# Copying the second half of w_in on VectorE instead of by DMA, each piece placed behind the work that it follows in time

## The chip, the cores and the metric

The kernel runs on one core of one Trainium2 chip. The metric is the device time of one execution in microseconds (us). A profile gives the span from the first to the last instruction, which is about 1.7 us shorter than the time of the same execution. Engines: PE is TensorE (matmuls), PEld its weight loads, DVE is VectorE, ACT is ScalarE, POOL is GpSimd, SP is SyncE, which here only issues DMAs. The kernel's matmuls write their results into tiles in PSUM; copying them from there into tiles in SBUF is called eviction below.

In the views below, rows left out are marked by "...".

## The reference, cut to what matters

A causal convolution of 7 taps over the sequence (weights by softmax, one set for each of 8 groups of 24 channels), then an MLP with the activation h * sigmoid(beta * h):

```python
# x: 8 x 4096 x 192, weight: 8 x 7
out = np.einsum('hk,bskhg->bshg', softmax(weight), windows_of_7(x))
x = out.reshape(32768, 192)
h = x @ w_in                                  # 192 x 2048
g = h * (1.0 / (1.0 + np.exp(-beta * h)))
return g @ w_out                              # 2048 x 192
```

## The kernel before: the parts that the change touches

The 192 channels are cut into NG = 3 chunks of 64. Two halves of the batch are worked on together: partitions 0 to 63 hold a chunk of the first half, partitions 64 to 127 the same chunk of the second. The kernel keeps w_in in SBUF twice, once for each set of partitions, and its matmuls read w_in from the same partitions as x. It is loaded in four pieces of 512 columns from HBM into partitions 0 to 63 (GpSimd issues these DMAs and they cast to bf16), and then copied inside SBUF to partitions 64 to 127. Piece 0 is copied by VectorE; pieces 1 to 3 by DMAs that SyncE issues.

```python
NW = 4
FW = F // NW                                   # 512 columns a piece
w_in_s = consts.tile([128, NG, F], BF16)

def load_w_in(i):
    cols = slice(i * FW, (i + 1) * FW)
    nc.gpsimd.dma_start(out=w_in_s[0:DG, :, cols], in_=moe_w_in[:, cols]...)

def second_w_in(i):
    cols = slice(i * FW, (i + 1) * FW)
    return dict(out=w_in_s[DG : 2 * DG, :, cols], in_=w_in_s[0:DG, :, cols])

load_w_in(0)
# ... cut ...
load_x(nc.gpsimd, x1b, TOK, 0, NB)
for i in range(1, NW):
    load_w_in(i)
    nc.sync.dma_start(**second_w_in(i))        # waits for load_w_in(i)
# ... w_out loads, cut; later, in VectorE's order:
nc.vector.tensor_copy(**second_w_in(0))
```

The main loop works in steps. Step s computes the hidden block `hidden(s, u)` for u = 0 to 15 (128 columns of w_in each, so blocks 4, 8 and 12 are the first to need pieces 1, 2 and 3) and, between them, the output of step s - 1. VectorE computes the convolution of a later step as 21 "taps" (`tensor_scalar` for the first of each chunk, `scalar_tensor_tensor` for the others). In step 0 there is no output yet; some start-up work is put between its hidden blocks:

```python
def hidden(s, fc):
    ph = psum_h.tile([128, 2, TOK], FP32, name="ph")       # 2 buffers
    for j in range(NG):
        for h in range(2):                                 # h = 1 reads the copied half
            rows = slice(h * DG, (h + 1) * DG)
            nc.tensor.matmul(ph[:, h, 0:n], w_in_s[rows, j, cols], cts[s][rows, j, 0:n], ...)
    nc.scalar.activation(gs[s][:, fc, :, 0:n], ph[:, :, 0:n], AF.Silu, scale=beta[:, fc : fc + 1])

first_work = {
    1: more(xt1_work),      # transposes of the next chunk of x, on TensorE
    3: more(xt1_work),      # the rest of them, and VectorE takes them out of PSUM
    5: more(conv1_work),    # convolution of step 1, one chunk of channels, on TensorE
    8: more(conv1_work),
    11: more(conv1_work),   # the last chunk, and VectorE takes it out of PSUM
}
```

GpSimd scales w_out by 1/beta (`prep_w_out`, four operations of 128x768) during step 0. The kernel gives each engine its instructions as one stream, in the order in which they were written.

## Time and profile before

| | before |
|---|---|
| time, median of 3 runs | 706.83 us (706.76 to 709.17) |
| span of the profiled run | 705.6 us |
| TensorE busy | 688.8 us, 98% |
| VectorE, ScalarE busy | 547.4 us, 577.8 us |
| longest wait of TensorE | 7.68 us, at 15.35 us |

From the page of the kernel before, the busy times of the engines and the group of the hidden matmuls (columns: line, engine, operation, output<-inputs, shapes, count; then busy us and mean ns; then idle time before them and what ended most of it):

```profile
PE 688.8 (98%) x11465; PEld 529.3 (75%) x11465; DVE 547.4 (78%) x932; ACT 577.8 (82%) x543; POOL 70.5 (10%) x83
L364 PE MATMUL ph<-ct,w_in_s 64*128 64x512 bf16 (+1 forms) x3168 | 427.0, 370 | 9.8 <-DMA w_in_s<-w_in_s 7.7
```

TensorE is the limit, and it idles 705.6 - 688.8 = 16.8 us in all. The second line says where nearly half of that is: 7.7 us in front of hidden matmuls, ended by the DMA that copies w_in from w_in.

The timeline of TensorE of the kernel before, start-up and the beginning of step 1 (start us, duration us, engine, line, what, count, and idle time before it):

```profile
14.61 0.53 PE L237 MATMUL po<-ident_b,x1b 128*64 128x128 bf16 x12
15.07 0.28 PE L364 MATMUL ph<-ct,w_in_s 64*128 64x256 bf16 x1
23.04 1.46 PE L364 MATMUL ph<-ct,w_in_s 64*128 64x256 bf16 x11 [7.68 <-DMA w_in_s<-w_in_s]
24.43 1.86 PE L250 MATMUL po<-xt_148,diag 128*128 128x256 f32 x7
...
28.25 1.10 PE L250 MATMUL po<-xt_148,diag 128*128 128x256 f32 x7
...
34.60 0.50 PE L364 MATMUL ph<-ct,w_in_s 64*128 64x256 bf16 x6 [0.20 <-ACT g L371]
34.92 0.51 PE L395 MATMUL po<-w_out_s,g 64*128 64x192 bf16 x8
```

At 15.07 the fifth hidden block (u = 4) issues one matmul, which needs only the first half of piece 1, and then stands for 7.68 us. Note the two convolution chunks: 1.86 us after the hole, 1.10 us later for the same seven matmuls. Step 1 begins at 34.60.

The table by stretches of the kernel before explains the 1.86 us (stretch; length, then busy us and instruction count of PE, PEld, DVE, ACT, POOL; then the granted TensorE clock, the DMA share and GB/s):

```profile
15.00:17.00 2.00, 0.35 (x7) 0.09 (x1) 1.78 (x5) 0.41 (x1) 0.00 (x0) 0.92 1.02 309
17.00:19.00 2.00, 0.00 (x0) 0.00 (x0) 2.00 (x3) 0.00 (x0) 1.82 (x1) 0.50 1.10 317
23.00:25.00 2.00, 1.97 (x13) 1.30 (x14) 0.00 (x0) 1.11 (x2) 2.00 (x2) 0.50 1.02 69
25.00:27.00 2.00, 2.00 (x17) 1.58 (x16) 0.00 (x0) 0.22 (x1) 2.00 (x3) 0.52 1.03 66
27.00:29.00 2.00, 1.56 (x20) 1.16 (x15) 0.00 (x0) 1.91 (x3) 2.00 (x4) 1.00 2.14 144
```

The granted clock falls to 0.50 in the hole and stays there until about 27, so the first 4 us of work after the hole run at a granted clock of 0.50. This is counted as busy time, not as waiting.

The timeline of VectorE of the kernel before:

```profile
9.97 0.76 DVE L286 COPY w_in_s<-w_in_s 64x1536 bf16<-64x1536 bf16 x1
...
15.18 0.96 DVE L315 COPY xt<-po 128x1536 bf16<-128x1536 bf16 x1 [2.92 <-PE po L237]
16.18 0.88 DVE L345 TENSOR_SCALAR ct<-xt,cw 128x512 bf16<-128x512 bf16 x3
16.97 2.62 DVE L347 SCALAR_TENSOR_TENSOR ct<-xt,cw,ct 128x512 bf16<-128x512 bf16 x2
32.14 0.96 DVE L301 CAST ct<-po 128x768 bf16<-128x768 f32 x1 [12.56 <-PE po L250]
```

A copy of one piece by VectorE takes 0.76 us; the same copy by DMA took 8.8 us to landing (median of three, table of DMA issues). VectorE idles from 19.6 to 32.1.

The chain of work that ended last, before, in order of time, passes the same stretch by another way:

```profile
10.23 12.57 DMA w_out_raw<-in_moe_w_out_dram
22.88 1.41 POOL w_out_s L321
24.28 3.54 DMA xd<-in_x_dram
27.82 0.49 PE ph L364 x6
```

It names the loads of w_out and of x and not the copy of w_in. Its link at 27.82 is a TensorE wait of 0.44 us that was put down to a DMA of x, which a hidden matmul does not read. The chain is inferred from semaphore events, and one wrong link sends everything before it astray. So "the DMA engines are too busy for w_out and x" is a rival reading of this profile.

### The profile page before, as it was taken

How to read it: one execution, taken by the hardware profiler on the slowest of the kernel's cores; microseconds unless marked ns; L12 is line 12 of the kernel's file. 1: busy time of each engine (PE TensorE's matmuls, PEld its weight loads, DVE VectorE, ACT ScalarE, POOL GpSimd, SP SyncE). 2: the span in 40 equal slices, each digit the busy share in tenths (PEclk: the TensorE clock that was granted, in tenths of full speed). 3: DMA queues.
4: the chain of work that ended last, by engine and by line, in shares of the span. 5: the costliest groups of instructions: out<-in, count | busy, mean ns of one | idle time of the engine just before them, and what ended most of it. 6: DMA issues, size and time to landing. Idle time of an engine off the chain costs nothing.

```text
span 705.6 us, 24846 instructions
## 1 busy us (share of the span) xinstructions
PE 688.8 (98%) x11465; PEld 529.3 (75%) x11465; DVE 547.4 (78%) x932; ACT 577.8 (82%) x543; POOL 70.5 (10%) x83
## 2 busy tenths in 40 slices
PE   7699999999999999999999999999999999999996
PEld 5487777777777777777777777777777777777776
DVE  5299999999798877788877779877778887777213
ACT  4499888888888888888888888888888888888881
POOL 6954544000000000000000000000000000000000
PEclk9799999999999999999999999999999999999999
DMA  9999999922212221421223220232221322111011
GB/s 178 155 161 161 159 168 177 139 57 60 69 44 51 69 71 47 69 59 35 69 70 49 69 69 32 63 69 65 52 70 48 47 69 70 47 47 47 24 47 69
DMA packets 182073, 55.16 MB, mean 78 GB/s; under 512 B 146432, under 2 KB 181648, under 8 KB 181968
## 3 DMA queue, kind: packets, MB, share of 16 engines
q0 software_dynamic: 98048, 14.89, 29.9%
q1 hardware_dynamic: 83872, 38.68, 24.3%
q8 instruction: 89, 1.46, 0.8%
q14 instruction: 16, 0.13, 0.1%
q10 hardware_dynamic: 48, 0.01, 0.0%
HBM read 28.98 MB, written 37.29 MB: 94 GB/s over the span
## 4 chain that ended last, share of the span: by engine, by line
PE 95%; DMA 2%; POOL 1%; ACT 0%; issue 0%; DVE 0%; POOLq 0%
PE po L395 48%; PE ph L364 47%; DMA w_out_raw<-in_moe_w_out_dram 2%; DMA xd<-in_x_dram 1%; ACT g L371 0%; POOL w_in_s L142 0%; POOL w_out_raw L185 0%; PE po L250 0%; POOL x1b L117 0%; POOL w_out_s L321 0%; DVE osb L404 0%; DVE osb L405 0%; POOL sel L158 0%; POOL sel L167 0%; POOL sel L156 0%
## 5 line engine op out<-in xcount | busy, mean ns | idle before, releaser
L371 ACT ACTIVATE g<-ph,beta 128x1024 bf16<-128x1024 f32 (+1 forms) x528 | 571.5, 1088 | 106.2 <-PE ph L364 102.3
L395 PEld LDWEIGHTS <-g 64*128 64x128 bf16 x8192 | 370.2, 94 | 101.3 <-issue 0.4
L364 PE MATMUL ph<-ct,w_in_s 64*128 64x512 bf16 (+1 forms) x3168 | 427.0, 370 | 9.8 <-DMA w_in_s<-w_in_s 7.7
L395 PE MATMUL po<-w_out_s,g 64*128 64x192 bf16 x8192 | 430.3, 243 | 0.2 <-issue 0.2
L347 DVE SCALAR_TENSOR_TENSOR ct<-xt,cw,ct 128x512 bf16<-128x512 bf16 x558 | 380.6, 747 | 0.0
L364 PEld LDWEIGHTS <-w_in_s 64*128 64x128 bf16 x3168 | 164.1, 94 | 63.5 <-DMA w_in_s<-w_in_s 7.9
L404 DVE COPY osb<-po 128x384 f32<-128x384 f32 x128 | 71.4, 558 | 129.3 <-PE po L395 123.3
L405 DVE TENSOR_TENSOR osb<-po,osb 128x384 f32<-128x384 f32 x128 | 71.4, 558 | 4.4
L95 POOL DMA_DIRECT2D xd<-in_x_dram x60 | 54.3, 906 | 49.6 <-DMA xd<-in_x_dram 46.5
L345 DVE TENSOR_SCALAR ct<-xt,cw 128x512 bf16<-128x512 bf16 x93 | 27.5, 349 | 0.0
L301 DVE CAST ct<-po 128x768 bf16<-128x768 f32 x1 | 1.0, 958 | 12.6 <-PE po L250 12.6
L321 POOL TENSOR_TENSOR w_out_s<-w_out_raw,beta_r 128x768 bf16<-128x768 f32 x4 | 6.6, 1674 | 3.1 <-DVE ct L345 2.6
L250 PE MATMUL po<-xt_148,diag 128*128 128x256 f32 x28 | 5.2, 332 | 0.0
L205 PE MATMUL ph<-zeros 128*128 128x512 bf16 x8 | 3.8, 625 | 1.3 <-DVE warm L132 1.3
L250 PEld LDWEIGHTS po<-xt_148,diag 128*128 128x128 f32 x28 | 4.3, 223 | 0.9 <-issue 0.8
L250 PEld LDWEIGHTS ph<-xt_148,diag 128*128 128x128 f32 x14 | 2.9, 303 | 0.7 <-ACT xt_148 L271 0.6
L250 PE MATMUL ph<-xt_148,diag 128*128 128x256 f32 x14 | 3.4, 406 | 0.0
L315 DVE COPY xt<-po 128x1536 bf16<-128x1536 bf16 x1 | 1.0, 958 | 2.9 <-PE po L237 2.9
L185 POOL DMA_DIRECT2D w_out_raw<-in_moe_w_out_dram x4 | 3.1, 789 | 0.0
L262 ACT CAST ct<-po 128x256 bf16<-128x256 f32 x1 | 0.4, 372 | 3.1 <-PE po L250 3.1
L205 PEld LDWEIGHTS <-zeros 128*128 128x128 bf16 x8 | 0.9, 129 | 2.5 <-issue 1.3
L142 POOL DMA_DIRECT2D w_in_s<-in_moe_w_in_dram x4 | 2.6, 676 | 0.8 <-POOLq L464 0.8
(45 smaller groups left out, 26.3 us busy)
## 6 DMA issues: line engine op xcount, KB each, us to landing
out_dram<-osb SPq DMA_DIRECT2D x62, 384.0 KB, 3.0
xd<-in_x_dram POOLq DMA_DIRECT2D x54, 198.0 KB, 14.7
w_out_raw<-in_moe_w_out_dram POOLq DMA_DIRECT2D x4, 384.0 KB, 9.9
xd<-in_x_dram POOLq DMA_DIRECT2D x6, 192.0 KB, 14.6
x_83<-in_x_dram SPq DMA_DIRECT2D x4, 192.0 KB, 4.0
w_in_s<-in_moe_w_in_dram POOLq DMA_DIRECT2D x4, 192.0 KB, 7.9
out_dram<-osb SPq DMA_DIRECT2D x4, 192.0 KB, 5.8
w_in_s<-w_in_s SPq DMA_DIRECT2D x3, 192.0 KB, 8.8
```

The costliest lines, as they stand in the source:

```text
L95: nc.gpsimd.dma_start(out=xd[r0:, :, h, :], in_=x_v[p, t0:t1, h, :].rearrange("t (c d) -> t c d", c=NG),)
L185: nc.gpsimd.dma_start(out=w_out_raw[:, c : c + 4, :], in_=w_out_v[:, c : c + 4, :])
L205: nc.tensor.matmul(pf[:, 0, :], zeros[:, 0:128], zeros, start=True, stop=True)
L250: nc.tensor.matmul(pv, diag[:, c, k, :], xt0[:, c, o : o + n], start=(k == 0), stop=(k == K - 1),)
L321: nc.gpsimd.tensor_tensor(w_out_s[:, c0 : c0 + n, :], w_out_raw[:, c0 : c0 + n, :], beta_r[:, c0 : c0 + n].unsqueeze(2).to_broadcast((128, ...
L345: nc.vector.tensor_scalar_mul(dst, src, scalar)
L347: nc.vector.scalar_tensor_tensor(out=dst, in0=src, scalar=scalar, in1=dst, op0=ALU.mult, op1=ALU.add)
L364: nc.tensor.matmul(ph[:, h, 0:n], w_in_s[rows, j, cols], cts[s][rows, j, 0:n], start=(j == 0), stop=(j == NG - 1),)
L371: nc.scalar.activation(gs[s][:, fc, :, 0:n], ph[:, :, 0:n], AF.Silu, scale=beta[:, fc : fc + 1])
L395: nc.tensor.matmul(po[:, r, b * D : (b + 1) * D], g[rows, fc, h, q * BLK : (q + 1) * BLK], w_out_s[rows, fc, :], start=(fc == 0), stop=(fc ...
L404: nc.vector.tensor_copy(dst, po[:, 0, 0 : 2 * D])
L405: nc.vector.tensor_tensor(dst, po[:, 1, 0 : 2 * D], dst, ALU.add)
```

## The change

Intent: take the second DMA out of the path. VectorE copies a piece in under 1 us. As VectorE works in order, each copy is placed where its piece should have landed: copy 1 behind the first transposes (u = 1), copy 2 behind the eviction of the transposes (u = 3), copy 3 at u = 5.

```diff
-    def second_w_in(i):
+    def copy_w_in(i):
         cols = slice(i * FW, (i + 1) * FW)
-        return dict(out=w_in_s[DG : 2 * DG, :, cols], in_=w_in_s[0:DG, :, cols])
+        nc.vector.tensor_copy(w_in_s[DG : 2 * DG, :, cols], w_in_s[0:DG, :, cols])
@@
     for i in range(1, NW):
         load_w_in(i)
-        nc.sync.dma_start(**second_w_in(i))
@@
-    nc.vector.tensor_copy(**second_w_in(0))
+    copy_w_in(0)
@@
-        1: more(xt1_work),
-        3: more(xt1_work),
-        5: more(conv1_work),
+        1: lambda: (more(xt1_work)(), copy_w_in(1)),
+        3: lambda: (more(xt1_work)(), copy_w_in(2)),
+        5: lambda: (more(conv1_work)(), copy_w_in(3)),
```

## The prediction

> **What bounds the kernel.** TensorE: the page gives it 688.8 us busy of 705.6 (98%), and the table by stretches shows no idle time from 50 to 700 us, at a granted clock of 1.00. So only the first 45 us can be won. The one large hole is at 15.35 us: the timeline shows the fifth hidden block's first matmul at 15.07 and the next at 23.04, after 7.68 us of waiting (list of waits) for the DMA that copies the second half of w_in, piece 1. SyncE issued it at 13.40, when piece 1 itself had landed; it took about 9.6 us. The hole costs more than itself: the granted clock is 0.50 from 17 to about 27 us. [...]
>
> **Removed, added, moved.** Three DMA copies of 192 KB go (median 8.8 us to landing). Three VectorE copies like the one already there come: 0.76 us each (timeline), 2.3 us together. VectorE works in order:
> - copy 1 waits for piece 1 (13.4) and ends near 14.2, before the work it feeds (15.1); it holds up only a halo cast and the transposes' eviction, which can't start before 15.18.
> - copies 2 and 3 follow that eviction (ends 16.14): to about 16.9 and 17.7, or 1 to 2 us later. Their pieces have landed by 16; their readers come near 18 and 22.
> - then five convolution taps (16.2 to 19.6 before). VectorE had idled from 19.6 to 32.1, so there is room.
>
> **On the critical path.** TensorE goes on at 15.07 at full clock. From pieces of the trace at full clock: two hidden blocks to 16.1; one convolution chunk to the next 2.75 us (28.25 to 31.00; the cold one 3.82); from the second chunk to the next step 6.35. So step 1 starts near 25.2 instead of 34.60: 9.4 us earlier, 7.7 of it the wait, about 1.7 the cold clock. Nothing else then binds: w_out is ready by 24.4, needed near 27; the first DMA-transposed x chunk lands about 34.5, needed near 36.
>
> **What may be given back.** After the second step's convolution is copied, VectorE has 16 taps of 0.67 us and an eviction, just as long as TensorE's step 1 (10.8 us), so a later start of VectorE reappears there. GpSimd scales w_out from 17 to 24 us: two taps took 2.62 us beside it, not 1.35. [...] Copies and taps now fall into that stretch: I take off 0.3 us. Gain 9.1 us.
>
> **Prediction: 697.7 us, range 696.2 to 700.5.** Faster by over 2% (below 692.7): 0.02. Within 2%: 0.97. Slower by over 2%: 0.01.
>
> **Signs.** Right: no TensorE wait on w_in over 0.5 us; granted clock about 1.0 from 10 to 30 us; step 1's first matmul on g near 25; four VectorE copies of w_in of about 0.76 us (one perhaps longer beside GpSimd); steady stretches unchanged. Wrong: TensorE waiting for a VectorE copy; a clock still at 0.5; a new hole of over 1 us at the start of steps 1 to 3, on VectorE's convolution or a late transposed chunk.
>
> **What would make it wrong.** Piece 1 landing after 15 us, since VectorE then delays the eviction too; [...] or the transposed chunks, whose DMA is saturated until 140 us, becoming the limit once TensorE starts earlier: then the gain shrinks towards 5 us.

The sum is 9.4 us (7.7 for the wait and about 1.7 for the cold clock, both from the trace of the kernel before) less 0.3 us, an estimate from the two taps that took 2.62 us beside GpSimd: 9.1 us off 706.83, so 697.7 us. "Saturated until 140 us" stands for the DMA share in the table by stretches of the kernel before: 1.90 to 2.26 from 30 to 140 us, 0.21 from 140 to 200.

## The result, and the profile after

| | before | after |
|---|---|---|
| time, median | 707.87 us (4 runs, 706.76 to 709.17) | 697.80 us (4 runs, 696.94 to 697.89) |
| span of the profiled run | 705.6 us | 696.1 us |
| TensorE busy | 688.8 us | 687.0 us |
| mean granted clock | 0.991 | 1.0 |

The ratio is 0.9854, with a 95% interval of 0.9831 to 0.9878: 1.5% faster. It is the mean time of one kernel over that of the other in the same rounds, so it is not quite the ratio of the medians. The 706.83 us that the prediction started from was the median of the first three runs.

From the page of the kernel after:

```profile
PE 687.0 (99%) x11465; PEld 527.4 (76%) x11465; DVE 552.9 (79%) x935; ACT 578.0 (83%) x543; POOL 70.3 (10%) x83
L363 PE MATMUL ph<-ct,w_in_s 64*128 64x512 bf16 (+1 forms) x3168 | 426.0, 370 | 2.6 <-ACT g L370 1.4
```

The two pages already split the gain. TensorE's idle time went from 705.6 - 688.8 = 16.8 us to 696.1 - 687.0 = 9.1 us, which is 7.7 us less. Its busy time fell by 1.8 us for the same 11,465 matmuls; the clock is the reason that the tables by stretches show. 7.7 + 1.8 = 9.5 us, the difference of the spans. Not all of the 7.7 us is the hole, though: the hole of 7.68 us went, small waits of 0.2 us in all came, and the remaining 0.3 us lie behind the last matmul. From there to the end of the span it was 5.5 us before and 5.3 after, and between 5.0 and 5.5 in all traces, so these 0.3 us can't be told from scatter. The last matmul itself ended at 700.1 before and at 690.9 after, 9.25 us earlier.

The timeline of TensorE after (the part that answers to the one before):

```profile
14.98 0.89 PE L363 MATMUL ph<-ct,w_in_s 64*128 64x256 bf16 x12
15.80 1.09 PE L249 MATMUL po<-xt_145,diag 128*128 128x256 f32 x7
...
18.54 1.11 PE L249 MATMUL po<-xt_145,diag 128*128 128x256 f32 x7
...
25.03 0.50 PE L363 MATMUL ph<-ct,w_in_s 64*128 64x256 bf16 x6 [0.33 <-DVE ct L300]
25.36 0.49 PE L394 MATMUL po<-w_out_s,g 64*128 64x192 bf16 x8
...
36.68 0.39 PE L363 MATMUL ph<-ct,w_in_s 64*128 64x512 bf16 x2 [0.27 <-DVE ct L346]
```

The hole is gone, all convolution chunks take 1.1 us, and step 1's first output matmul comes at 25.36 instead of 34.92: 9.56 us earlier. Two small new waits have appeared, both on VectorE (0.33 and 0.27 us).

The table by stretches after:

```profile
17.00:19.00 2.00, 1.55 (x21) 1.11 (x18) 1.97 (x2) 1.61 (x3) 2.00 (x2) 1.00 1.33 275
...
23.00:25.00 2.00, 1.17 (x16) 0.53 (x11) 2.00 (x3) 1.98 (x4) 2.00 (x3) 1.00 0.02 1
```

The clock is 1.00 in every stretch from 11 to 37 us. VectorE, which idled here before, is now busy without a break from 15.1 us on. Its timeline after:

```profile
13.25 0.69 DVE L149 COPY w_in_s<-w_in_s 64x1536 bf16<-64x1536 bf16 x1 [1.20 <-DMA w_in_s<-in_moe_w_in_dram]
...
16.08 2.54 DVE L149 COPY w_in_s<-w_in_s 64x1536 bf16<-64x1536 bf16 x2
18.65 1.70 DVE L344 TENSOR_SCALAR ct<-xt,cw 128x512 bf16<-128x512 bf16 x3
20.28 3.82 DVE L346 SCALAR_TENSOR_TENSOR ct<-xt,cw,ct 128x512 bf16<-128x512 bf16 x2
24.02 0.94 DVE L300 CAST ct<-po 128x768 bf16<-128x768 f32 x1
```

Copies 2 and 3 took 2.54 us instead of 1.4, the three first taps 1.70 instead of 0.88, the two others 3.82 instead of the 1.40 that two such taps take later in the same trace: together 8.1 us for about 3.7 us of work. GpSimd scales w_out from 16.6 to 23.6 in this trace. The chain of work that ended last, after, in order of time, shows what that means:

```profile
16.08 2.55 DVE w_in_s L149 x2
18.65 1.70 DVE ct L344 x3
20.36 3.75 DVE ct L346 x2
...
32.65 3.98 DVE ct L346 x6
36.63 0.04 issue
36.68 0.39 PE ph L363 x2
```

From 15.1 to 36.7 us the start of step 2 hangs on VectorE alone in this trace, though TensorE waits for it only 0.33 and 0.27 us. VectorE and TensorE now finish the start-up nearly together: in the second trace of this kernel (after_again, below) TensorE does not wait for VectorE at all.

### The profile page after: what moved, and what is told of

The parts are those of the page before. It is cut to its first block, busy times and chain, and to the rows that moved or that the text cites. A ratio compares the mean times of both kernels' runs of the same rounds, so it can differ in the third digit from the quotient of the medians.

```text
span 696.1 us, 24845 instructions
## 1 busy us (share of the span) xinstructions
PE 687.0 (99%) x11465; PEld 527.4 (76%) x11465; DVE 552.9 (79%) x935; ACT 578.0 (83%) x543; POOL 70.3 (10%) x83
## 3 DMA queue, kind: packets, MB, share of 16 engines
q0 software_dynamic: 98048, 14.89, 29.7%
q8 instruction: 89, 1.46, 0.9%
## 4 chain that ended last, share of the span: by engine, by line
PE 96%; DVE 3%; ACT 0%; issue 0%
PE po L394 48%; PE ph L363 46%; DVE ct L346 2%; PE ph L204 1%; PE ph L249 0%; DVE w_in_s L149 0%; PE po L236 0%; DVE ct L344 0%; PE po L208 0%; ACT g L370 0%; DVE osb L404 0%; DVE osb L403 0%; PE po L249 0%; DVE xt L314 0%; DVE ct L300 0%
## 5 line engine op out<-in xcount | busy, mean ns | idle before, releaser
L149 DVE COPY w_in_s<-w_in_s 64x1536 bf16<-64x1536 bf16 x4 | 4.0, 1015 | 1.3 <-DMA w_in_s<-in_moe_w_in_dram 1.2
(45 smaller groups left out, 26.4 us busy)
```

The source lines that it names most:

```text
L149: nc.vector.tensor_copy(w_in_s[DG : 2 * DG, :, cols], w_in_s[0:DG, :, cols])
```

## The experiments

Theory: the gain is TensorE's wait for a DMA that stood behind another DMA, plus the half clock that the wait brought on, less a little that VectorE gives back. Rivals: all of it is the wait and the clock costs nothing; or the DMA traffic that was saved, for w_out and x; or the place of the copies doesn't matter, as VectorE had 12.6 idle us. The runs came in three calls. Only runs of one call share a chip and the runs of the kernel before, whose median was 708.10, 708.06 and 706.83 us there.

### 1. The saved traffic put back: same_traffic

```diff
+    spare = setup.tile([128, NG, F], BF16)
     for i in range(1, NW):
         load_w_in(i)
+        cols = slice(i * FW, (i + 1) * FW)
+        nc.sync.dma_start(
+            out=spare[DG : 2 * DG, :, cols], in_=w_in_s[0:DG, :, cols]
+        )
```

> The kernel after, with the three SBUF-to-SBUF DMAs of 192 KB still issued by SyncE behind their pieces, but into a spare tile that nobody reads. Theory (the gain is the wait and the clock, not the traffic): within 0.7 us of 697.8. Rival (the DMA engines were freed for w_out and x, and that brought part of the gain): slower by 2 us or more, with w_out or the transposed chunk late.

Measured: 697.64 us median (697.21 to 698.17), ratio to before 0.9853 against 0.9854 for the change. The same three DMAs, issued from 13.8 us on (13.4 in the kernel before), cost nothing when nobody waits for them. So the traffic is not the cause, and the reading that the chain of before suggested falls.

### 2. One piece only: first_piece_only

```diff
     for i in range(1, NW):
         load_w_in(i)
+        if i > 1:
+            nc.sync.dma_start(out=w_in_s[DG : 2 * DG, :, cols], in_=w_in_s[0:DG, :, cols])
@@
-        3: lambda: (more(xt1_work)(), copy_w_in(2)),
-        5: lambda: (more(conv1_work)(), copy_w_in(3)),
+        3: more(xt1_work),
+        5: more(conv1_work),
```

> The kernel after, but only piece 1 of w_in is copied by VectorE; pieces 2 and 3 go by DMA as before. The profile of before names a wait for one copy alone. Theory: the wait for piece 2 was only hidden behind that for piece 1; its copy would land near 22.5 and is needed at 18.1, so a hole of 4 to 4.5 us opens at the ninth hidden block, perhaps with a cold clock after it: about 702.5 us (701 to 704). Rival (only the wait that the profile named counts): 697.8 us.

Measured: 702.79 us (702.10 to 704.06), ratio 0.9932. TensorE's timeline of this run:

```profile
17.88 0.27 PE L368 MATMUL ph<-ct,w_in_s 64*128 64x256 bf16 x1 [0.45 <-ACT g L375]
22.10 0.82 PE L368 MATMUL ph<-ct,w_in_s 64*128 64x256 bf16 x5 [3.95 <-DMA w_in_s<-w_in_s]
```

The wait moved to the ninth hidden block, where piece 2 is first needed, and the clock fell to 0.50 again, from 19.3 to 26.2 us. The profile of before named one wait, but a second one stood behind it. Removing only the named wait would have brought half.

### 3. All copies in one place: all_early

```diff
-    copy_w_in(0)
+    for i in range(NW):
+        copy_w_in(i)
     diag_conv(0, 2, ...)
# and no copies in first_work
```

> The kernel after, with all four VectorE copies in one place, where the first one stands, before the last convolution chunk's eviction. Theory (VectorE works in order, so a copy that waits for its DMA holds up what follows): the copies wait until about 15.5, the first hidden block starts near 16.5 instead of 12.2, with a cold clock after the idle time: 702 to 704 us. Rival (2.3 us of copies are cheap wherever they stand): 697.8 us within 0.7.

Measured: 704.24 us (704.03 to 704.58), ratio 0.9947, just above the range. VectorE waited 3.72, 0.53 and 0.22 us for the three pieces, and TensorE waited 5.29 us for the convolution chunk that VectorE took out of PSUM only after them (17.30 instead of 10.76):

```profile
17.77 1.03 PE L364 MATMUL ph<-ct,w_in_s 64*128 64x256 bf16 x8 [5.29 <-DVE ct L263]
```

The clock fell too, to 0.50 from 16.2 to 23.0 us. So the place of the copies is worth about two thirds of the change: 6.4 of 10 us (6.6 of 10.5 where same_traffic stands for the change).

### 4. Wait and clock apart: warm_hole, then hole_busy and hole_idle

warm_hole is the kernel before with dummy matmuls in its hole:

```diff
+        if s == 0 and fc == 4:
+            for _ in range(35):
+                nc.tensor.matmul(ph[:, 0, :], zeros[:, 0:128], zeros, start=True, stop=True)
```

> The kernel before, with 35 dummy matmuls of 128x512 put on TensorE exactly where its 7.68 us hole is (before the fifth hidden block of step 0, into the PSUM buffer that this block then overwrites). The wait for the DMA copy stays, only the clock is kept up. Theory (wait 7.7 us plus a cold clock of 1.7 to 1.9 us after it): granted clock 1.0 through the hole, restart still near 23, step 1's first matmul on g near 33.1 instead of 34.9, span about 703.8 against 705.6. Rival (the clock costs nothing, all of the gain is the wait): span unchanged within 0.5 us.

Measured: 707.42 us (705.32 to 708.46), ratio 0.9987 with an interval of 0.9969 to 1.0006. This did not decide, and the trace says why:

```profile
22.56 0.28 PE L367 MATMUL ph<-ct,w_in_s 64*128 64x256 bf16 x1
25.19 0.82 PE L367 MATMUL ph<-ct,w_in_s 64*128 64x256 bf16 x11 [2.35 <-DMA w_in_s<-w_in_s]
```

The copy landed at 25.19, 2 us later than in the profile of before, so a wait of 2.35 us was left, and soon after it the clock fell anyway, to 0.50 from 26.5 to 30.0 us. A wait for a DMA is a poor ruler, as its length is not fixed. So two kernels were made from the kernel after, with a hole of given length. In hole_busy TensorE has 35 dummy matmuls ahead of the sixth hidden block:

```diff
+        if s == 0 and fc == 5:
+            for _ in range(35):
+                nc.tensor.matmul(ph[:, 0, :], zeros[:, 0:128], zeros, start=True, stop=True)
```

In hole_idle ScalarE has 12 dummy activations, so that the sixth hidden block waits, idle, for its PSUM buffer:

```diff
+        if s == 0 and fc == 3:
+            for _ in range(12):
+                nc.scalar.activation(spare, zeros, AF.Silu)
         nc.scalar.activation(gs[s][:, fc, :, 0:n], ...)
```

> The kernel after, with 35 dummy matmuls of 128x512 ahead of the sixth hidden block of step 0 (about 7.7 us, as they measured in the run warm_hole): the delay of the old hole without idle TensorE time and without any wait for a DMA. Together with hole_idle it prices the cold clock, which warm_hole could not, as there the DMA copy landed 2 us later than in the profile of before. Theory: clock 1.0 throughout; 7.7 us later than the kernel after, less up to 1 us that VectorE's chain to step 2 stops costing: 704.5 to 705.5 us. Rival (no clock cost): the same as hole_idle within 0.5 us.

> The kernel after, with 12 dummy activations of 128x512 on ScalarE ahead of the fourth activation of step 0, so that TensorE's sixth hidden block waits about 7.5 us for its PSUM buffer, idle. Theory: the clock falls to 0.5 in the hole and for 3 to 4 us after it, which costs 1.7 to 1.9 us more than hole_busy at the same length of hole: 706 to 707.5 us. Rival (no clock cost): the same as hole_busy within 0.5 us.

Measured: hole_busy 704.09 us (703.69 to 704.87), clock 0.999 to 1.0; hole_idle 706.78 us (706.48 to 707.40), clock 0.992 to 0.995. TensorE's timelines, hole_busy and then hole_idle, show that the sixth hidden block began at almost the same time:

```profile
23.25 0.50 PE L366 MATMUL ph<-ct,w_in_s 64*128 64x256 bf16 x6
```

```profile
23.02 0.82 PE L364 MATMUL ph<-ct,w_in_s 64*128 64x256 bf16 x6 [7.16 <-ACT g L374]
```

So the clock has a price of its own: 2.7 us between the medians (and 2.7 between the means, 704.18 and 706.86), 1.6 us between the two profiled runs, whose times were 704.87 and 706.48. The trace accounts for the smaller figure: in hole_idle the clock stood at 0.50 from 19.6 to 26.4, so that 3.4 us of work after the hole ran cold, which by estimate costs half of that, 1.7 us. The rest of the 2.7 us is not shown. The rival that the clock costs nothing falls. hole_busy came out 0.4 us below its range. It cost 6.3 us between the medians, and 7.05 between the profiled spans, for dummy work of 7.7. Part of the rest was slack: the two waits for VectorE of the kernel after (0.33 and 0.27 us) are not in this trace. What else the medians hide is not shown.

### 5. Both kernels again: before_again and after_again

No edit.

> The kernel before, unchanged, for a second trace on another chip. In warm_hole the DMA copy of piece 1 landed at 25.2 instead of 23.0. Theory (the landing of that copy varies between executions, and the time of the kernel with it): TensorE's hole is 8 to 10 us here and the span as much over 705.6 as the hole is over 7.7. Rival (the hole is the same and the time varies elsewhere): 7.7 us within 0.3.

> The kernel after, unchanged, on the chip of the next runs, for their comparison and for a second trace. Theory: no TensorE wait on w_in, 697.8 us within 0.5, copies and taps between 16 and 24 us stretched differently from execution to execution[...].

Measured: before_again 708.65 us, one run, state unknown, span 706.9; after_again 697.88 us (696.72 to 698.10), clock 0.999 to 1.0 in all four runs. TensorE's timeline of before_again:

```profile
23.40 1.46 PE L364 MATMUL ph<-ct,w_in_s 64*128 64x256 bf16 x11 [8.33 <-DMA w_in_s<-w_in_s]
```

The expectation was half right. The hole was 0.65 us longer than in the first profile, but the span was 1.3 us longer. The other half is busy time of TensorE, 689.5 instead of 688.8 us, for which the clock is the likely reason. In the first profile of before it fell at 16.7 and rose at 26.9; in before_again it fell at 19.5 and rose at 29.7. Both cold stretches last 10.2 us, but they lie differently to the hole, so that after it 3.9 us of work ran cold in one and 6.3 us in the other. In after_again, three pieces of the theory held: no wait on w_in, the time within 0.1 us, and the operations beside GpSimd stretched differently (the three first taps took 2.91 us there, 1.70 in the first trace of after). Why they do was not shown. But there step 1 did not wait for VectorE:

```profile
25.08 0.50 PE L363 MATMUL ph<-ct,w_in_s 64*128 64x256 bf16 x6 [0.20 <-ACT g L370]
```

Nor did step 2, and the chain of work that ended last runs through TensorE and ScalarE from 14 to 40 us, with one pause of TensorE of 0.75 us at 32.2 for which the profile names no cause. The times, 698.10 and 697.81 us, are nearly the same.

### 6. Is VectorE's new work free? double_copies

```diff
-        3: lambda: (more(xt1_work)(), copy_w_in(2)),
-        5: lambda: (more(conv1_work)(), copy_w_in(3)),
+        3: lambda: (more(xt1_work)(), copy_w_in(2), copy_w_in(2)),
+        5: lambda: (more(conv1_work)(), copy_w_in(3), copy_w_in(3)),
```

> The kernel after, with copies 2 and 3 each done twice on VectorE (1.4 us more work, up to 2.5 us where GpSimd holds it up). The chain of the profile after runs through VectorE from 15.1 to 36.7 us, copies and taps, to step 2. Theory (that chain now sets the start of step 2): slower by 1.2 to 2.5 us, with a TensorE wait on the last tap at the start of step 2 that grows by as much. Rival (the VectorE work is free, there were 12.6 idle us): within 0.4 us of the kernel after.

Measured: 698.93 us (698.15 to 699.70), about 1.1 us slower than the kernel after (ratios to before 0.9868 and 0.9854, whose intervals overlap). It was run at another time. The time is just under the range and not resolved by itself, but the trace agrees with the theory: the last part of step 2's first hidden block started at 37.74 instead of 36.68. The growth was not where I expected it. TensorE's wait at the start of step 1 grew from 0.33 to 1.19 us; the one on the last tap stayed at 0.27. So the copies are close to the critical path, in spite of the 12.6 us that VectorE had idled before.

### 7. Two attempts to shorten VectorE's chain: prep_on_vector and early_second

prep_on_vector moves the scalings of w_out from GpSimd to VectorE:

```diff
-        nc.gpsimd.tensor_tensor(
+        nc.vector.tensor_tensor(            # in prep_w_out
@@
-    for c in range(0, NF, 4):
-        prep_w_out(c, 4)
@@  in first_work
+        7: lambda: prep_w_out(0, 4),
+        9: lambda: prep_w_out(4, 4),
+        12: lambda: prep_w_out(8, 4),
+        13: lambda: prep_w_out(12, 4),
```

> The kernel after, with the four scalings of w_out moved from GpSimd to VectorE, between its taps in step 0, so that nothing on GpSimd computes while VectorE copies. Theory (GpSimd and VectorE hold each other up: copies, taps and scalings took 8.1 us of VectorE for 3.7 us of work): the copies are back at 0.7 us each and the taps at 0.3 and 0.67; the four scalings cost VectorE about 0.85 us each, 3.4 us, less than the 4.4 us it loses now, so VectorE reaches step 2 about 1 us earlier and the kernel gains 0.3 to 1.0 us: 696.8 to 697.5. Rival (the slow operations are slow for another reason, as DMA writes): they stay slow, and the kernel is 2 to 3 us slower.

Measured: 697.97 us (697.77 to 698.38), ratio 0.9855: no gain and no loss, 0.5 us above the range. VectorE's timeline:

```profile
16.22 1.68 DVE L149 COPY w_in_s<-w_in_s 64x1536 bf16<-64x1536 bf16 x2
...
19.30 0.66 DVE L342 TENSOR_SCALAR ct<-xt,cw 128x512 bf16<-128x512 bf16 x2
...
20.75 1.40 DVE L344 SCALAR_TENSOR_TENSOR ct<-xt,cw,ct 128x512 bf16<-128x512 bf16 x2
```

The two taps that took 3.82 us after are back at 1.40, and the copies near 0.8 each. So it was mainly GpSimd's scalings that stretched them; the three first taps, at 0.59 us for one and 0.66 for two, still took more than the 0.88 of the kernel before. By which mechanism was not shown. But the four scalings cost VectorE 0.94 us each, 3.8 us, about what the stretching had cost. Its last tap of the chain ended at 36.9 us here and 36.6 after. The time was only moved.

early_second puts copy 2 directly behind copy 1:

```diff
-        1: lambda: (more(xt1_work)(), copy_w_in(1)),
-        3: lambda: (more(xt1_work)(), copy_w_in(2)),
+        1: lambda: (more(xt1_work)(), copy_w_in(1), copy_w_in(2)),
+        3: more(xt1_work),
```

> The kernel after, with copy 2 directly behind copy 1, ahead of the eviction of the transposes, in time in which VectorE was idle (0.65 us). Theory (VectorE's chain from 15.1 us on sets the start of step 2): up to 0.7 us faster than after_again if piece 2 has landed by then, 0.3 slower if it lands late and holds up the eviction: 697.1 to 698.1 us. Rival (VectorE is free): no difference.

Measured: 698.73 us median of four runs, above the range, slower than after_again on the same chip by 0.85, and in two groups: 697.88 and 697.92 us at a clock of 0.999 or more, 699.54 and 700.18 at 0.995. The profiled run (699.54) shows what happened. Piece 1 landed at 14.1 and piece 2 at 15.7 us in it, so copy 2 held up the eviction of the transposes to 16.56. The three first taps took 4.13 us beside GpSimd, VectorE was late for step 1, and TensorE waited for it:

```profile
25.83 0.82 PE L363 MATMUL ph<-ct,w_in_s 64*128 64x256 bf16 x6 [1.33 <-DVE ct L300]
```

These six matmuls took 0.82 us and not 0.50: this wait of 1.33 us, with one of 0.46 us shortly before it, was enough to bring the clock down to 0.50, from 25.8 to 29.2 us. One of the four runs of double_copies, the slowest (699.70), also has a clock of 0.995; its profiled run, with a wait of 1.19 us, kept the clock. The placement that the change chose, copy 2 behind the eviction, was no slower than two of these four runs and about 2 us faster than the other two; the intervals of the two ratios to before (0.9879 and 0.9862) overlap.

### 8. A DMA, but not behind another: both_from_hbm

```diff
     for i in range(1, NW):
         load_w_in(i)
+        nc.gpsimd.dma_start(
+            out=w_in_s[DG : 2 * DG, :, cols],
+            in_=moe_w_in[:, cols].rearrange("(c d) f -> d c f", c=NG),
+        )
# and no copies in first_work
```

> The kernel after, with the second half of pieces 1 to 3 loaded from HBM by DMA a second time, next to the first half, instead of copied. Theory (what cost the kernel before was one DMA behind another, two landings in a row, not the use of a DMA as such): the second half of piece 1 lands near 15, and TensorE waits under 1.5 us for w_in in all; but w_out and x queue behind 0.6 MB more, 1 to 3 us later: 698 to 701 us. Rival (any DMA copy of this size is too slow): near the kernel before, over 704 us.

Measured: 698.42 us (698.14 to 698.63), ratio 0.9872; after_again, on the same chip, 697.88. No wait on w_in is left in the trace, with all three second halves loaded by DMA. These loads took about as long as the old copies (the seven loads of w_in by DMA landed after 8.4 us in the median, the copies after 8.8), but GpSimd issued them at 6.7, 7.9 and 9.1 us and not from 13.4 on. So a DMA was not too slow for this; a DMA that can start only when another has landed was. The 0.5 us to the kernel after went as the theory said: the scalings of w_out ran from 20.6 to 27.2 instead of 16.6 to 23.6, into step 1, where ten taps took 9.12 us instead of 6.70.

No kernel here was faster than the kernel after clear of the noise (same_traffic's 697.64 us is 0.2 below it).

## Why the prediction was right

- **What bounds the kernel.** Right. The page after still shows TensorE at 99%, and all of the gain but the 0.3 us behind the last matmul came in the first 37 us.
- **The wait, 7.7 us.** Right: the hole of 7.68 us is gone. That TensorE's idle time in all also fell by 7.7 us is partly chance, as small waits came (0.2 us) and the end of the span was 0.3 us shorter.
- **The cold clock, about 1.7 us.** Right in kind and near in size: the busy time fell by 1.8 us. hole_busy and hole_idle show it as a cost of its own, 1.6 to 2.7 us. It is not a fixed number, as before_again shows.
- **The place of the copies.** Right: copy 1 ended at 13.94 (14.2 predicted), copies 2 and 3 at 18.6 (17.7, or 1 to 2 us later), and no matmul waited for them. all_early shows that this had to be got right.
- **Step 1 near 25.2, 9.4 us earlier.** Right: the step's first hidden block began at 25.03 instead of 34.60, and its first output matmul 9.56 us earlier.
- **What is given back, 0.3 us.** Right: 9.56 us earlier at the first output matmul of step 1, 9.25 at the first one behind step 2's first hidden block (36.89 instead of 46.14) and still 9.25 at the last matmul, so 0.3 us went back during step 1. In this trace it went in the way that was named: GpSimd and VectorE held each other up, and TensorE waited 0.27 us for VectorE's last tap. In after_again that wait is missing and the pause of 0.75 us stands there instead, so the way is not the same in every execution.
- **When the clock falls.** In the trace of the kernel before the clock fell 1.35 us after the idle time began. In before_again it took 4.4 us, and in early_second waits of 0.46 and 1.33 us sufficed. What was regular is the length of the cold stretches; see the last section.
- **The time.** Predicted 697.7 us, measured 697.80. The closeness is partly luck. The prediction took 9.1 us off 706.83; the gain was 9.25 us up to the last matmul, 9.5 between the profiled spans and 10.1 between the medians, as the kernel before has executions up to 709.6 us, which I did not allow for. In eight runs of the kernel after (two calls) the times are 696.72 to 698.10; the kernel before in the same two calls ranges from 705.84 to 709.17. That removing the DMA wait narrowed this is what two traces of before suggest (landing at 23.0 and 23.4, different cold stretches); it was not shown run by run.

Left open: why the copy lands at 23.0 in one execution and at 25.2 in another. In the trace of warm_hole, SyncE could issue it only at 14.3 instead of 13.4, so 0.9 of the 2.2 us lies in the load of piece 1; the rest was not followed up.

## What to carry to other kernels

Where an engine waits for a DMA that itself waits for another DMA, break the pair: copy on an idle engine, or load twice from HBM; either brought nearly all of the gain here (697.80 us by the copies, 698.42 by the loads), and the traffic itself cost nothing (same_traffic, 697.64 us). Place the new instructions in the engine's order where their data has landed (all_early, with all of them in one place, lost 6.4 us), and look for a second wait behind the one that the profile names. Price a hole in TensorE as its length plus the half-clock stretch that it may bring on (1.6 to 2.7 us between hole_busy and hole_idle), and before filling another engine's idle time look at what that engine must finish next.

## What the traces show of the clock, of VectorE beside GpSimd, and of the DMAs

- **The clock.** It fell 1.35 us (before) and 4.4 us (before_again) after the idle time began, and in early_second at the end of a wait of 1.33 us, when TensorE had been busy for 1.01 of the 2 us before 25.0. So in that run a wait of 1.33 us, with one of 0.46 us shortly before it, cost the clock. Waits of 0.33 (after) and 1.19 us (double_copies) at the same place did not.
- **How long it stayed down.** By tables with stretches of a quarter of a us, the cold stretches of the start-up lasted 3.41 us (early_second, warm_hole), 6.83 us (first_piece_only, all_early, hole_idle) and 10.24 us (before, before_again), that is, one, two or three times 3.41 us, wherever the work resumed. In the 3.41 us before the clock fell, TensorE had been idle for 1.42 us (before), 1.64 (first_piece_only), 1.8 (early_second), 2.06 (warm_hole) or all of it (all_early, hole_idle, before_again). In the 3.41 us before it rose, TensorE had been idle for at most 0.14 us in all seven. In before_again it stayed at 1.00 at 16.05, after 3.41 us with 1.05 us idle, and at 0.50 at 26.29, after 3.41 us with 0.53 us idle. How much idle time it takes, and what sets the lengths, was not shown.
- **VectorE beside GpSimd.** Two taps took 3.82 us beside GpSimd (after) and 1.40 without (prep_on_vector). The same three first taps took 0.88 us alone (before) and 1.70, 2.91, 4.13 and 4.50 us beside GpSimd in after, after_again, early_second and same_traffic. GpSimd lost time too: in the trace of before its two scalings that began while VectorE's taps ran took 1.86 and 1.90 us, the other two, with VectorE idle, 1.46 and 1.47.
- **The DMAs.** Beside other traffic here, GpSimd's loads of w_in (192 KB each) took 7.9 us in the median to landing, and the copies of the same size, issued by SyncE, 8.8. Such a time, read from a trace with the traffic beside it, is what a plan needs.
